# A sparse-attention and feed-forward kernel whose planner hands out PSUM banks by age, with a new order of all engines' work

## The chip, the cores and the metric

The kernel runs on one core of one Trainium2 chip. The metric is the device time of one launch in microseconds (us); below, "time" is this figure, and "span" is the stretch from the first to the last instruction in one profiled execution. The core's engines are named as in the profile: PE (TensorE, matrix products), DVE (VectorE), ACT (ScalarE), POOL (GpSimd), and SP, which here issues DMA transfers. Each engine works through its own list of instructions in order, and waits for others by semaphores. PE's results go to PSUM, a small store of eight banks of 512 float32 columns on 128 partitions, from which ACT or DVE must fetch them before a bank can be filled again.

## The reference

Four batches of eight heads, 768 positions, head size 64. Attention is masked by blocks of 32: neighbours, first and last block, and three sampled blocks for each query block. The result, 3,072 tokens of 512 values, goes through two weight matrices with a squared ReLU between them. Masking and softmax are in the attention part, relu and square in the second:

```python
scores = scale * np.matmul(q, k.transpose(0, 1, 3, 2))
scores = np.where(mask, scores, -1000000000.0)
scores = scores - np.max(scores, axis=-1, keepdims=True)
attn = np.exp(scores)
attn = attn / (np.sum(attn, axis=-1, keepdims=True) + 1e-09)
attn_out = np.matmul(attn, v)
x = attn_out.transpose(0, 2, 1, 3).reshape(B * S, H * D)
h = x @ w_in            # 512 -> 2048
r = np.maximum(h, 0.0)
g = r * r
return g @ w_out        # 2048 -> 512
```

## The kernel before

**Work and tiles.** Heads go in pairs: 16 pairs ("units"), four for each batch. For a pair, q and k are loaded as float32, cast to bf16 (`qc`), and transposed into `QK`: for the first batch by PE through PSUM (`transp`, `evac`), later by DMA (`transp_dma`, L402). v is cast into `VT`. Scores (L443) are computed with the keys on the partitions, 256 queries by two chunks of 128 keys for each of the two heads, which fills both banks of one X tile. ACT takes the exponential into `pT` (L454), DVE multiplies by a 0/1 mask (`MK`, L461), and PE multiplies with v (L483), with a column of ones that gives the sum. DVE normalises (L491, L493), and the result is transposed into `xT`. For the first 256 queries of the first batch the mask is added on PE instead (L447).

The second half takes a tile of 128, 256 or 384 tokens at a time. `hidden` (L541) fills one bank (512 columns; tiles of 128 and 256 tokens) or both banks of an X tile (768 columns; tiles of 384), in two or four parts. `relu` (L550 on ACT, L552 on DVE) brings it to SBUF as float32 `r`, `square` (L560 on ACT, L562 on POOL) makes `g`, and `output` (L585) multiplies by the second matrix, 16 matmuls for 128 tokens, into a bank of its own (`py`). A copy to `ys` (L246 on ACT, L248 on DVE or POOL) and a store end it.

**PSUM.** Three tiles X0 to X2 of 1,024 float32 columns, two banks each, are the shared store: scores and wide hidden groups need a whole tile ("X2" in the planner, two cells), and narrow hidden groups, first-batch transposes, mask tiles (L365) and some last outputs need one bank ("X1", one cell). One more bank serves `po`, one `py`.

**What sets the order.** The order is not written out. Every piece of work is a `Task` with a duration for each engine that may do it, a key (its rank), what it depends on, and the buffers that it takes (`get`) and gives back (`put`). `run_schedule` (L107) simulates the engines: again and again it takes the ready task that could start first, ties broken by the key, and emits it; so this model decides every engine's order, which engine does a piece, and which cells it uses. To the keys is added a pseudo-random number (`tie`, scaled by `TIES`, from one seed for every 64 tasks in `SEEDS`). `AHEAD` lets an urgent task be waited for. `LEAD` says how long before a unit's first scores its casts may begin, `PACE0` and `PACE` when each score group of the later batches may start. `arrive` lists when the model believes each load of the first batch to have landed. `bias` adds to a candidate engine's end when engines are compared, so a larger `bias` for ACT gives more of that work to DVE or POOL.

The function `bank` (L135) chooses a cell for a task that takes X1 or X2. Cells still held are left out; among the others the smallest `k_` wins: first the time `r` at which the task could use it, which is `now` for every cell that is free already, then, for one bank, a cell whose neighbour in the same tile is held, then the lowest number.

Of the kernel before, what the change touches and what calls it, by code (L numbers as in the profile page):

```python
# [25 lines left out]
def kernel(  # L26
# [21 lines left out]
    HP = H // 2  # L48
# [31 lines left out]
    LAT = {"PE": 0.23, "DVE": 0.06, "ACT": 0.06, "POOL": 0.08, "SP": 1.4}  # L80
    OVER = {"PE": 0.0, "DVE": 0.08, "ACT": 0.09, "POOL": 0.03, "SP": 0.0}
    SWITCH, SHARE, SLACK = 0.096, 0.85, 0.1
    AHEAD = {"PE": 0.043, "DVE": 0.108, "ACT": 0.176, "POOL": 0.0, "SP": 0.0}
    LEAD = 5.943
    HOLD = 0
    PACE0, PACE, SINGLE, MASK_AT = 39.28, 1.726, 1, 17.0

# [1 line left out]
    class Buf:  # L91
        def __init__(self, pool):
# [2 lines left out]

    TIES = 2.583, 1.777
    SEEDS = (
            621053, 621053, 621053, 162164, 486097, 621053, 621053, 88936, 279485,  # L100
            617998, 621925, 997023, 39474, 741514, 621053, 644142, 104467, 983473,
            256392, 272690, 973551, 604649, 254998, 99264)

    def tie(n):
        x = (n + 1) * 2654435761 & 0xFFFFFFFF ^ SEEDS[n // 64] * 2246822519 & 0xFFFFFFFF
# [18 lines left out]
    def run_schedule(free, bufs, dma_free, mode=128):  # L124
# [12 lines left out]
        def bank(pool, now, gone):  # L137
            n = 2 if pool == "X2" else 1
            best = None
            for c in range(0, 6, n):  # L140
                mine = [cells[i] for i in range(c, c + n)]
                if any(i in gone for i in range(c, c + n)) or any(b and b.holds for b in mine):
                    continue
                r = max([now] + [b.free for b in mine if b])
                o = cells[c ^ 1]
                k_ = (round(r, 4), n == 1 and not (o and o.holds), c)
                if best is None or k_ < best[0]:
                    best = (k_, c, r)
            return best

        relaxed = False
        while waiting or ready:
# [5 lines left out]
            now = [t for t in waiting if all(d.end is not None for d in t.deps)]  # L158
# [310 lines left out]
    def po_pool(u, q0):  # L469
        return "y" if u < HP and q0 < QW and (u + q0 // P) % 2 else "po"  # L470
# [127 lines left out]
    def T_(engs, key, f, *args, **kw):  # L598
        return Task(engs, key, (lambda e: f(*args, e)), **kw)
# [1 line left out]


    arrive = {(0, 1, 0): 3.4, (0, 0, 0): 4.2, (0, 1, CP): 4.55, (1, 0, 0): 5.7, (1, 1, 0): 6.7, (2, 0, 0): 7.2, (2, 1, 0): 8.3, (0, 2, 0): 9.4,
              (3, 0, 0): 9.8, (3, 1, 0): 10.9, (1, 2, 0): 12.4, (2, 2, 0): 13.5, (3, 2, 0): 14.6}
    arrive.update({(u, 0, 2): (15.5, 16.2, 16.8, 17.5)[u] for u in range(HP)})

    KEYS_OF = {P: [tuple(range(CP)), tuple(range(CP, NCH))], QW: [(2 * c, 2 * c + 1) for c in range(CP)]}
    OPEN = [(0, 0), (0, 1), (1, 0), (2, 0), (1, 1), (3, 0), (2, 1), (3, 1)]
# [56 lines left out]
    def attend(group, add):  # L665
        s = min(order.index(a) for a in group)
        bufs = {a: Buf("X2") for a in group}
        area = sum(a[2] * len(a[3]) for a in group) / 512
        deps = [ev[a[0]][1, n] for a in group for n in a[3]]
        deps += [ev[a[0]][0, n] for a in group for n in range(a[1] // P, (a[1] + a[2]) // P)]  # L670
        sc = T_(("PE", (0.44 if add else 0.22) * area), s, scores, group, add, bufs,
                deps=deps + (mr[:1 + (group[-1][1] + group[-1][2] > QW)] if add else []) + sc_all[-1:], get=[bufs[a] for a in group], mode=64,
                after=PACE0 + PACE * (s - N0) * (1.06 - 0.0006 * (s - N0)) if s >= N0 else 0.0, paced=group[0][1] >= QW or s >= N0)
        sc_all.append(sc)
        for i, a in enumerate(group):
            u, q0, w, cs = a
            sc_of[u].append(sc)
            s = order.index(a)
            part = w * len(cs) / 512
            pt = Buf("pT")  # L680
            ex = T_(("ACT", 0.2 + 0.82 * part), s, exps, a, deps=[sc], lead=sc.engs["PE"] * (len(group) - 1 - i) / len(group), get=[pt], put=[bufs[a]])
            if not add:
                ex = T_(("DVE", 0.68), s - 1, masks, a, deps=[ex] + [mk[n, c] for n in cs for c in range(q0, q0 + w, P)], port=True)
            if cs[0] == 0:
                ob[u, q0] = Buf(po_pool(u, q0))
            va = T_(("PE", 0.245 * part), s + 2.023, values, a, deps=[ex] + cv[u] + va_all[-1:] + (kws if po_pool(u, q0) == "y" else []),
                    get=[] if cs[0] else [ob[u, q0]], put=[pt], mode=128)
            va_all.append(va)
            va_of[u].append(va)
            if cs[-1] == NCH - 1:  # L690
                b, a_ = divmod(u, HP)
                by_dma = b > 0
                xqb = Buf("xq")
                nm = T_(("DVE", 0.3 + 0.16 * w / P), s - 9, normalize, u, q0, w, deps=[va], get=[xqb], put=[ob[u, q0]] if by_dma else [])
                kw = {}
                if b not in xb:
                    xb[b] = Buf("xT")
                    kw = dict(get=[xb[b]])
                if by_dma:
                    mu[u, q0] = T_(("SP", 1.22), s - 9, x_transp_dma, u, q0, w, deps=[nm], put=[xqb], dma=0.6, **kw)  # L700
                    continue
                xt = T_(("PE", 0.06 * w / P), s - 9, x_transp, u, q0, w, deps=[nm], put=[xqb], mode=128)
                mu[u, q0] = T_({"DVE": 0.11 + 0.09 * w / P, "ACT": 0.2 + 0.09 * w / P}, s - 9, x_evac, u, q0, w, deps=[xt], put=[ob[u, q0]], **kw)
# [10 lines left out]
    kws = []  # L714
# [28 lines left out]
    for k_, T in enumerate(TILES + [None]):  # L743
        hs = [(T, f) for f in range(0, NF, per_unit(T))] if T else []
        ys = [(TILES[k_ - 1], i, part) for i in range(len(y_tiles(TILES[k_ - 1]))) for part in range(NY)] if k_ else []
        both = [((i + 0.5) / len(hs), 0, x) for i, x in enumerate(hs)]
        both += [((i + 0.5) / len(ys), 1, x) for i, x in enumerate(ys)]
        for _, kind, x in sorted(both, key=lambda z: z[:2]):
            n_key += 1
            t = x[0]  # L750
            b, c0, w = t
            if kind == 0:
                f = x[1]
                need = [mu[b * HP + a, q0] for a in range(HP) for q0, qw in QT[b] if q0 < c0 + w and c0 < q0 + qw]
                w *= per_unit(t)
                wide = w > 512
                hb, rb = Buf("X2" if wide else "X1"), Buf("r")
                last_use = c0 + t[2] == S and f + per_unit(t) == NF
                parts = 4 if wide else 2
                hd = []  # L760
                for part in range(parts):
                    end = part == parts - 1
                    hd.append(T_(("PE", HID[w] / parts), n_key - (0.6 if part else 0.5), hidden, t, f, part, parts, hb,
                                 deps=hd[-1:] or need + [wl[f * NWP // NF], wl[(f + per_unit(t) - 1) * NWP // NF]],
                                 get=[] if part else [hb], put=[xb[b]] if last_use and end else [], mode=128, yields=not part))
                h1 = hd[-1]
                rr = T_(RELU[w], 200, relu, t, f, deps=[h1], get=[rb], put=[hb], bias={"ACT": 0.092})
                n = 1 if wide else per_unit(t)
                for i in range(0, per_unit(t), n):
                    gb = Buf("g")  # L770
                    gbuf[t, f + i + n - 1] = gb
                    sq = T_(SQ[n * t[2]], n_key, square, t, f, i, n, deps=[rr], get=[gb], put=[rb], bias={"ACT": 0.673})
                    sq_of.update({(t, f + i + j): sq for j in range(n)})
            else:
                _, i, part = x
                ts, cs = y_tiles(t)[i]
                n = (cs[1] - cs[0]) / d_model
                fs = range(part * NF // NY, (part + 1) * NF // NY)
                if part == 0:
                    yb = Buf(y_pool(t, i))  # L780
                last_i = i == len(y_tiles(t)) - 1
                yy = T_(("PE", 0.432 * n), n_key, output, t, i, ts, cs, part, yb,
                        deps=[sq_of[t, f] for f in fs] + [wl[NWP + f * NWP // NF] for f in fs] + ([yprev] if part else []),
                        get=[] if part else [yb], put=[gbuf[t, f] for f in fs if (t, f) in gbuf] if last_i else [], mode=128)
                yprev = yy
                if part == NY - 1:
                    sb = Buf("ys")
                    yc = T_({"ACT": 0.22 + 0.365 * n, "DVE": 0.15 + 0.53 * n}, 150, out_copy, t, i, cs, deps=[yy], get=[sb], put=[yb])
                    T_(("SP", 0.55), 0, store, t, i, ts, cs, deps=[yc], put=[sb], late=2.0, dma=0.7)
# [34 lines left out]
```

## Time and profile before

| what | us |
|---|---|
| time, median of 6 runs | 276.99 (276.83 to 278.73) |
| time of the profiled execution | 276.85 |
| its span | 275.1 |
| ACT busy, exponentials `pT` L454 | 137.9 (148 instructions) |
| ACT busy, relu L550 | 48.6 (65) |
| DVE busy, masks L461 | 93.3 (132) |
| PE, hidden L541 / output L585 to `py` | 640 / 328 matmul records |

The TensorE clock was granted in full throughout (1.000). Durations below come from the profiled execution, so a sum is made against its 276.85 us, of which 1.75 lie outside the span. Busy time on PE overlaps from one matmul to the next and some matmul records are missing, so PE's work is better read from start to start. A group's mean duration is taken by form where a line has several.

### The profile page before, as it was taken

To read this page: it belongs to the slowest core of one execution; us is meant where nothing else is said; L and a number is where in the kernel's file an instruction comes from. 1 tells how busy PE (TensorE), PEld (TensorE's weight loads), DVE (VectorE), ACT (ScalarE), POOL (GpSimd) and SP (SyncE) were. 2 spreads that over 40 slices of the span, in tenths; PEclk is the share of its full clock that TensorE was granted. 3 is DMA by queue.
4 is the path that set the end of the run, shared out by engine and by line. 5 is a ranking of instruction groups with operands and counts; after the bars stand their busy time and mean duration, and the time that the engine had idled before them with its cause. 6 is when DMAs were issued, how large, how long until landed. Compare 5 with 4: busy or idle time off the path is not lost.

```text
span 275.1 us, 7322 instructions
## 1 busy us (share of the span) xinstructions
PE 262.4 (95%) x2992; PEld 166.4 (61%) x3032; DVE 165.6 (60%) x339; ACT 224.2 (82%) x294; POOL 87.2 (32%) x110
## 2 busy tenths in 40 slices
PE   8989999889998999999999999999999999999995
PEld 5677665766566575556656556656565666555544
DVE  7777889734976988576847476685665555001010
ACT  3789999958997999999899989899798988646511
POOL 3192336345522035542221251312221122333210
PEclk9999999999999999999999999999999999999999
DMA  6999999999671239866670122443411011011112
GB/s 205 370 230 204 206 263 362 276 280 320 118 220 33 59 43 215 124 227 170 176 228 14 48 73 62 97 71 76 88 57 51 12 57 50 10 41 39 38 69 84
DMA packets 51881, 36.91 MB, mean 134 GB/s; under 512 B 30984, under 2 KB 48904, under 8 KB 51848
## 3 DMA queue, kind: packets, MB, share of 16 engines
q1 hardware_dynamic: 47080, 31.86, 43.5%
q0 software_dynamic: 4224, 4.19, 9.5%
q8 instruction: 23, 0.38, 0.5%
q10 hardware_dynamic: 544, 0.39, 0.5%
q14 instruction: 10, 0.08, 0.1%
HBM read 27.26 MB, written 6.29 MB: 122 GB/s over the span
## 4 chain that ended last, share of the span: by engine, by line
PE 86%; DVE 4%; ACT 3%; issue 2%; DMA 2%; SPq 1%; ACTq 0%; DVEq 0%
PE X L541 30%; PE py L585 27%; PE po L483 12%; PE X L443 12%; DMA ks<-in_k_dram 2%; PE X L585 2%; ACT r L550 1%; ACT pT L454 1%; DVE pT L461 1%; DVE QK L248 1%; SPq L274 1%; PE X L365 1%; PE po L500 1%; PE X L395 1%; PE X L447 0%
## 5 line engine op out<-in xcount | busy, mean ns | idle before, releaser
L454 ACT ACTIVATE pT<-X 128x1024 bf16<-128x1024 f32 (+1 forms) x148 | 137.9, 1006 | 8.1 <-PE X L443 5.3
L461 DVE TENSOR_TENSOR pT<-pT,MK 128x1024 bf16<-128x1024 bf16 x132 | 93.3, 727 | 24.4 <-ACT pT L454 23.7
L562 POOL TENSOR_TENSOR g<-r 128x384 bf16<-128x384 f32 (+1 forms) x65 | 59.2, 914 | 151.4 <-ACT r L550 129.5
L541 PE MATMUL X<-xT,w_in_sb 128*128 128x384 bf16 (+2 forms) x640 | 99.9, 294 | 2.9 <-ACT r L550 2.5
L585 PE MATMUL py<-w_out_sb,g 128*128 128x512 bf16 (+1 forms) x328 | 87.6, 374 | 3.4 <-issue 1.9
L541 PEld LDWEIGHTS <-w_in_sb 128*128 128x128 bf16 x640 | 54.3, 97 | 33.3 <-issue 6.7
L550 ACT ACTIVATE r<-X 128x768 f32<-128x768 f32 (+1 forms) x65 | 48.6, 754 | 22.4 <-PE X L541 19.7
L483 PEld LDWEIGHTS <-pT 128*128 128x128 bf16 x1152 | 47.4, 98 | 17.8 <-issue 4.2
L483 PE MATMUL po<-VT,pT 128*128 128x65 bf16 x1152 | 53.4, 194 | 0.1
L585 PEld LDWEIGHTS <-g 128*128 128x128 bf16 x400 | 34.3, 98 | 27.8 <-issue 4.4
L443 PE MATMUL X<-QK 64*128 64x256 bf16 (+1 forms) x624 | 46.8, 264 | 0.5
L443 PEld LDWEIGHTS <-QK 64*128 64x128 bf16 x624 | 26.1, 94 | 18.8 <-issue 14.2
L560 ACT ACTIVATE g<-r 128x384 bf16<-128x384 f32 (+1 forms) x55 | 29.7, 540 | 3.0 <-DVE r L552 1.4
L491 DVE RECIPROCAL rs<-po 128x4 f32<-128x4 f32 (+1 forms) x52 | 9.3, 178 | 35.7 <-PE po L483 35.6
L248 DVE COPY ys<-py 128x512 f32<-128x512 f32 x17 | 11.7, 685 | 27.6 <-PE py L585 27.6
L493 DVE TENSOR_TENSOR xq<-po,rs 128x256 bf16<-128x256 f32 (+1 forms) x52 | 21.0, 404 | 1.8
L248 POOL CAST VT<-vs 128x768 bf16<-128x768 f32 x15 | 15.7, 1048 | 18.7 <-issue 11.2
L248 DVE CAST qc<-ks 128x768 bf16<-128x768 f32 (+1 forms) x15 | 11.3, 755 | 0.8 <-DMA ks<-in_k_dram 0.7
L248 DVE CAST qc<-qs 128x768 bf16<-128x768 f32 (+2 forms) x16 | 9.1, 571 | 0.2 <-DMA qs<-in_q_dram 0.2
L246 ACT COPY ys<-py 128x512 f32<-128x512 f32 (+1 forms) x6 | 3.3, 558 | 5.5 <-PE py L585 5.3
L447 PE MATMUL X<-R,oh 64*128 64x128 bf16 x96 | 6.9, 219 | 0.0
L585 PE MATMUL X<-w_out_sb,g 128*128 128x512 bf16 (+1 forms) x32 | 6.0, 326 | 0.0
(54 smaller groups left out, 76.2 us busy)
## 6 DMA issues: line engine op xcount, KB each, us to landing
vs<-in_v_dram SPq DMA_DIRECT2D x16, 384.0 KB, 6.6
out_dram<-ys SPq DMA_DIRECT2D x23, 256.0 KB, 2.2
ks<-in_k_dram SPq DMA_DIRECT2D x15, 384.0 KB, 4.9
qs<-in_q_dram SPq DMA_DIRECT2D x12, 384.0 KB, 3.9
w_in_sb<-in_moe_w_in_dram POOLq DMA_DIRECT2D x4, 512.0 KB, 8.6
w_out_sb<-in_moe_w_out_dram POOLq DMA_DIRECT2D x4, 512.0 KB, 15.0
qs<-in_q_dram SPq DMA_DIRECT2D x4, 256.0 KB, 7.2
xT<-xq SPq DMA_TRANSPOSE x36, 2.3
```

What stands on the lines that cost most here:

```text
L248: (V if e == "DVE" else G).tensor_copy(out=out, in_=in_)
L443: nc.tensor.matmul(ps[:, h, j * w:(j + 1) * w], QK[i][hs, 1, ksl], QK[i][hs, 0, qsl], start=j == 0, stop=not add, skip_group_check=True)
L454: A.activation(out=pT[:, :, 0:n], in_=stile.pop(a)[:, :, 0:n], func=AF.Exp, scale=scale)
L461: V.tensor_tensor(out=pT, in0=pT, in1=m[:, None].broadcast_to([P, 2, len(cs), w]), op=AOP.mult)
L483: nc.tensor.matmul(po[:, qc, h, :], pT[:, h, j * w + qc * P:j * w + (qc + 1) * P], VT[i][:, h, n, 0:VW], start=(n == 0 and qc == 0 and h = ...
L491: V.reciprocal(out=rs, in_=po[:, :, :, D:VW])
L493: V.tensor_tensor(out=xq, in0=po[:, :, :, 0:D], in1=rs.broadcast_to([P, n, 2, D]), op=AOP.mult)
L541: nc.tensor.matmul(htile[T, f][:, i], w_in_sb[:, kc, (f + i) * P:(f + i + 1) * P], xT[b][:, kc, c0:c0 + w], start=(kc == 0), stop=(kc == K ...
L550: A.activation(out=to, in_=src, func=AF.Relu)
L560: A.activation(out=g, in_=r, func=AF.Square)
L562: (G if e == "POOL" else V).tensor_mul(out=g, in0=r, in1=r)
L585: nc.tensor.matmul(ytile[T, i], gtile[T, f][:, ts * P:(ts + 1) * P], w_out_sb[:, f, cs[0]:cs[1]], start=(f == 0), stop=(f == NF - 1))
```

## The change

In `bank`, the first term of the choice is no longer the time at which a cell can be used, but that of the cell's release plus 0.8 us, or `now` if that is later. Cells that came free over 0.8 us ago are equal; among fresher ones the one that was released first is taken. The time at which the task may start is worked out as before. The loads of v for units 1 to 3 and the second parts of q are believed to land 0.4 to 1.0 us later. The other numbers steer the model: `AHEAD`, `LEAD` (5.943 to 9.349), `PACE0`, the shift of the value matmuls' key, and ACT's biases for relu (0.092 to 0.192) and square (0.673 to 0.8). New `TIES` and `SEEDS` give a new order. All of these act before the program is built; none adds an instruction to it. Line numbers after `bank` grow by one.

```diff
-    AHEAD = {"PE": 0.043, "DVE": 0.108, "ACT": 0.176, "POOL": 0.0, "SP": 0.0}
-    LEAD = 5.943
+    AHEAD = {"PE": 0.045, "DVE": 0.057, "ACT": 0.278, "POOL": 0.0, "SP": 0.0}
+    LEAD = 9.349
     HOLD = 0
-    PACE0, PACE, SINGLE, MASK_AT = 39.28, 1.726, 1, 17.0
+    PACE0, PACE, SINGLE, MASK_AT = 40.983, 1.721, 1, 17.0
...
-    TIES = 2.583, 1.777
+    TIES = 1.511, 0.048
     SEEDS = (
-            621053, 621053, 621053, 162164, 486097, 621053, 621053, 88936, 279485,
...
+            309547, 309547, 309547, 309547, 65971, 309547, 309547, 729044, 629699,
...
                 r = max([now] + [b.free for b in mine if b])
                 o = cells[c ^ 1]
-                k_ = (round(r, 4), n == 1 and not (o and o.holds), c)
+                old = max([now] + [b.free + 0.8 for b in mine if b])
+                k_ = (round(old, 4), n == 1 and not (o and o.holds), c)
...
-              (3, 0, 0): 9.8, (3, 1, 0): 10.9, (1, 2, 0): 12.4, (2, 2, 0): 13.5, (3, 2, 0): 14.6}
-    arrive.update({(u, 0, 2): (15.5, 16.2, 16.8, 17.5)[u] for u in range(HP)})
+              (3, 0, 0): 9.8, (3, 1, 0): 10.9, (1, 2, 0): 13.4, (2, 2, 0): 14.5, (3, 2, 0): 15.4}
+    arrive.update({(u, 0, 2): (16.1, 16.7, 17.3, 17.9)[u] for u in range(HP)})
...
-            va = T_(("PE", 0.245 * part), s + 2.023, values, a, deps=[ex] + cv[u] + va_all[-1:] + (kws if po_pool(u, q0) == "y" else []),
+            va = T_(("PE", 0.245 * part), s + 2.994, values, a, deps=[ex] + cv[u] + va_all[-1:] + (kws if po_pool(u, q0) == "y" else []),
...
-                rr = T_(RELU[w], 200, relu, t, f, deps=[h1], get=[rb], put=[hb], bias={"ACT": 0.092})
+                rr = T_(RELU[w], 200, relu, t, f, deps=[h1], get=[rb], put=[hb], bias={"ACT": 0.192})
...
-                    sq = T_(SQ[n * t[2]], n_key, square, t, f, i, n, deps=[rr], get=[gb], put=[rb], bias={"ACT": 0.673})
+                    sq = T_(SQ[n * t[2]], n_key, square, t, f, i, n, deps=[rr], get=[gb], put=[rb], bias={"ACT": 0.8})
```

More of the change, by code (lines that the diff above doesn't have):

```diff
@@ L93, in __init__ @@
             self.pool, self.holds, self.free, self.at = pool, 0, 0.0, None
-    TIES = 2.583, 1.777
+    TIES = 1.511, 0.048
     SEEDS = (
-            621053, 621053, 621053, 162164, 486097, 621053, 621053, 88936, 279485,
-            617998, 621925, 997023, 39474, 741514, 621053, 644142, 104467, 983473,
-            256392, 272690, 973551, 604649, 254998, 99264)
+            309547, 309547, 309547, 309547, 65971, 309547, 309547, 729044, 629699,
+            29976, 309547, 521787, 731003, 309547, 309547, 787178, 309547, 792806,
+            298466, 671173, 309547, 137610, 309547, 309547)
     def tie(n):
```

## The prediction

> **What bounds the kernel now.** I read the page's busy line first, then the slices, the chain of waits, PE's waits, the windows by stage, and last the timeline around PE's longest stops.
>
> ```profile
> PE 262.4 (95%) x2992; PEld 166.4 (61%) x3032; DVE 165.6 (60%) x339; ACT 224.2 (82%) x294; POOL 87.2 (32%) x110
> ...
> PE   8989999889998999999999999999999999999995
> ...
> DVE  7777889734976988576847476685665555001010
> ACT  3789999958997999999899989899798988646511
> ...
> PE 86%; DVE 4%; ACT 3%; issue 2%; DMA 2%; SPq 1%; ACTq 0%; DVEq 0%
> ```
>
> PE is busy from the first slice to the last and carries 86% of the chain. Ninety-five per cent busy doesn't tell how much PE time could go, so I counted PE's work by its issue intervals. The chain shows them:
>
> ```profile
> 248.00 1.30 PE X L541 x8
> 249.30 2.16 PE py L585 x10
> ```
>
> That is 162 ns for a hidden matmul of 384 columns and 216 ns for an output of 512. In the same way, from start to start in the timeline: 109 ns for 256 columns, 56 for 128, 30 for a value matmul, 54 for each of a pair of 256-column score matmuls, and 190 ns extra for going into a run of scores and out again. Times their counts in the program (384 x 162, 128 x 109 and 128 x 56 hidden; 368 x 216 and 32 x 109 out; 1,152 x 30 values; the scores, transposes and masks) the products make 245.0 us, and 74 runs of scores add 13.9: **258.9 us**. I call the running sum of these PE's position. PE starts at 1.2 us and its last matmul goes out near 271.6, so some 11.6 us are stops. Setting each PE start in the trace against its position gives where: 4.0 us up to position 20, 3.8 from 20 to 50, 2.4 from 50 to 90, and 1.4 in the remaining 170 us. Beyond position 90 there is next to nothing to win.
>
> ```profile
> PE X L541 <- ACT r L550: 2.5, 4, 0.8
> ...
> 52.00:62.00 10.00, 8.20 (x85) 6.10 (x84) 4.65 (x9) 6.79 (x13) 5.05 (x5) 1.00 1.06 265
> ...
> 57.55 0.60 PE L541 MATMUL X<-xT,w_in_sb 128*128 128x256 bf16 x4
> 58.18 0.60 ACT L550 ACTIVATE r<-X 128x512 f32<-128x512 f32 x1 [0.50 <-PE X L541]
> 58.83 0.60 PE L541 MATMUL X<-xT,w_in_sb 128*128 128x256 bf16 x4 [0.69 <-ACT r L550]
> ```
>
> The first line (waiter, releaser, total us, times, longest) is PE's largest entry: four stops, at 53.55, 58.83, 60.11 and 85.69, which by starts cost 0.97 + 0.86 + 0.37 + 0.88 = 3.1 us. The window from 52 to 62 is where PE is least busy, and there ACT (6.79) and DVE (4.65) are idle too: nobody is overloaded, they take turns. The three timeline lines show how. Four matmuls, then ACT's relu, then the second four matmuls of the same group. In the built order that relu reads the other half of the X tile that PE is writing. It waits for PE's latest write to that tile, and PE's next part waits for the relu. So the two banks of one X tile are not independent in this program, although the planner's model keeps six separate cells.
>
> **What the Trainium skill says.** The Trainium skill, page "PSUM — Partial Sum Buffer", section "PSUM bank collisions raise a hardware error", asks for a guard by bank; reads and writes of different banks may run together. The trace shows a stricter guard here: PE at 58.83 waits 0.69 us for a read of the neighbouring bank. Its page "Perfetto Trace Analysis", section "Identifying the Most-Contended Engine", says that matmul busy time is a poor measure of headroom; I agree, and took issue intervals. Its page "ScalarE: Activation LUTs", section "Rules for kernel authors", wants relu on VectorE. Here the rows say otherwise for this operand: a 768-wide relu out of PSUM takes 958 ns on DVE (one case) and 812 on ACT.
>
> **The change, part by part.**
>
> *PE.* The same instructions, and 74 runs of scores in both: 258.9 us again. What differs is who waits.
>
> *Work moved between engines* (counts from both built orders, durations from the rows by form). ACT loses 14 relus of 768 columns (14 x 0.812), 3 of 512 (3 x 0.600), 3 squares (0.52 + 2 x 0.63) and one x copy, and gains 3 output copies (3 x 0.595) and one QK copy (some 0.4): -13.1 us. DVE gains 14 x 0.958 + 3 x 0.686 and loses 3 x 0.685 of output copies and a cast or so: +13.0. POOL gets some 2.6 more. This looks large and is worth little. Twelve of the fourteen wide relus come after the last scores, where slices 35 to 40 have DVE at 0 or 1 and ACT at 6 and below; there PE returns to a bank 3.4 to 5.6 us after filling it, against 0.96 for the relu. I cost them at nothing. Were that cover gone, each would cost its extra 0.15 us, 1.8 in all.
>
> *Which bank is taken.* For every PE wait on a reader of an X tile I took the room: PE work between the last matmul that the reader waits for and the waiting one. A wait has no margin when the room is under the reader's duration and some 0.3 us for the two signals; it is exposed to a short queue when under duration and 0.6.
>
> | PE position, us | waits exposed, before / after | sum short, before / after, us |
> |---|---|---|
> | 0-20 | 13 / 20 | 0.59 / 0.94 |
> | 20-50 | 10 / 10 | 1.58 / 1.59 |
> | 50-90 | 8 / 3 | 1.15 / 0 |
> | 90-259 | 22 / 9 | 0.15 / 0.54 |
>
> Four waits of before on the other half of a tile are short by 0.79, 0.79, 0.36 and 0.79, 2.73 us together; they are the four stops that the trace has at 3.08. After, those four are gone, and three new ones stand at positions 45.5, 48.4 and 49.8 with 0.68 + 0.36 + 0.44 = 1.48. At the same ratio of 1.13 they cost 1.67: **-1.4 us**. Elsewhere the start is worse by 0.35, and around position 116 a hidden group takes a bank with a room of 1.01 against an exp of 1.03, and three more are short by 0.08: **+0.35 and +0.4**.
>
> *Queues.* ACT is what PE waits for from 20 to 50 (19.58 us busy of 20 between 22 and 42). Adding up ACT's durations in order until the last instruction that PE needs gives, at position 38, 41.0 before and 39.4 after; at 50, 54.1 and 52.1; at 90, 94.1 and 92.5. Two of the 2.0 us at 50 are relus and squares that now stand later or on DVE. Some of the 6.2 us lost between 20 and 90 is that queue: 6.2 less the 3.1 of the four stops. Bounds: 0, if DVE takes ACT's place, and -2.0; I take **-0.8**, since the excess of ACT's sum over PE's position grows from 20 to 46 by 4.8 us before and 3.8 after.
>
> *Later landings in the model.* No instruction. They put v casts and values later in the start, where the trace has v of the second to fourth pair landing at 12.5, 13.5 and 14.8 us against 13.4, 14.5 and 15.4 in the new list: margin, within the start's +0.35. Bounds -0.5 and +1.5 (below).
>
> *Casts 3.4 us earlier (LEAD).* Smallest room from a batch's cast to the scores that use it: 9.3 us before, 9.9 after, against a transpose of 2.8 to landing. The loads have more than 10 us before any cast from the second batch on. Nothing. The last stores are issued in the same order, so the tail of 3.3 us stays.
>
> Sum: -1.4 + 0.35 + 0.4 - 0.8 = -1.45. The profiled execution took 276.85 us (span 275.1), 0.14 under the median of 276.99: **275.4 us**.
>
> **Rivals.**
> - *Stops only move, 276.6.* DVE's additions cancel the queue's gain and the start costs 0.7: -1.4 + 0.7 + 0.4 = -0.3. For it: banks free for over 0.8 us still tie, and the tie still goes to the half-held tile, so "oldest first" bites only on fresh banks; waits on a neighbour half even rise from 21 to 33. That is also the case that the change doesn't do what it says. Against: the rooms from 50 to 90.
> - *Slower, 278.7: DVE decides the start.* Its sum up to what PE needs is 27.2 after against 25.7 at position 22 (one more 768 cast, one more mask) and 43.4 against 40.3 at 38. DVE is busy 17.14 of 20 us from 22 to 42, so 2.9 us of idle time may cover it, or be waits that stay. If under 1.3 us of that idle time can be used, 1.5 us at 22 and 1.0 more by 38 come through: -1.4 + 0.35 + 0.4 + 2.5 = +1.85.
> - *All cover holds, 273.3.* From 20 to 90 only the three half-tile stops and 1.0 us of small waits remain of 6.2: -3.5.
>
> **How the numbers follow.** Forecast 0.46, stops move 0.22, slower 0.21, full cover 0.11. Changes under 0.5% (1.4 us) I count as none, about what a measurement of this kernel can tell. The forecast is at -0.57%, and I leave a fifth of its chance to no change: faster 0.37 + 0.11 = 0.48, same 0.22 + 0.09 = 0.31, slower 0.21. Its own range is 274.4 to 276.4; the full range takes in most of both outer cases, 273.4 to 278.4.
>
> **What would show it.** Right: no PE stop near 85 us, three between 50 and 62 of 0.2 to 0.6 us after r; PE's X waits on r from 2.5 to some 1.5 us; ACT near 211 and DVE near 179 us busy; POOL idle, tail and chain end as before. Wrong on the start: the first batch's hidden matmuls, which stand at position 20.4 after 19.9, begin later than about 26.3 us against 25.4, with DVE at 9 in the slices before. Wrong on the queue: the window from 22 to 42 loses more PE time than the 0.6 us of now. A stop of over 1 us beyond 100 us, or a DMA landing among PE's releasers, would upset the forecast altogether.

## The result, and the profile after

The changed kernel takes 278.43 us (median of 36 runs, 277.73 to 279.80); the kernel before, run beside it, 277.25 (73 runs). The ratio is 1.0039, with a 95% interval of 1.0029 to 1.0049: some 1.1 us slower, where 1.45 us faster was forecast. The profiled execution has a span of 276.6 us against 275.1. (One correction to the text above: in the listing `run_schedule` begins at L124 and `bank` at L137.)

The page of the changed kernel: the busy line, three of the slices, the chain.

```profile
PE 263.5 (95%) x2994; PEld 165.2 (60%) x3032; DVE 179.1 (65%) x353; ACT 211.1 (76%) x277; POOL 90.7 (33%) x113
...
PE   7899999789999999999999999999999999999995
...
DVE  7776999836997886767565657567576565434400
ACT  3779898746998999999879799998979988223111
...
PE 76%; ACT 7%; DVE 7%; DMA 3%; issue 3%; SPq 2%; POOL 1%; ACTq 0%; DVEq 0%
```

ACT and DVE stand where the counting put them (211 and 179), DVE partly by luck, as told below. The chain has changed: PE carries 76% of it in place of 86%, ACT and DVE together 14% in place of 7%. In the PE line the eighth slice (48 to 55 us) has a 7 in place of an 8.

PE's waits after 45 us in the changed kernel (waiter, releaser, total us, times, longest; the four largest), and then PE's timeline at the four stops that matter:

```profile
PE X L542 <- ACT r L551: 1.2, 2, 0.9
PE po L484 <- DVE xT L249: 0.9, 1, 0.9
PE po L484 <- DVE pT L462: 0.5, 1, 0.5
PE X L542 <- DVE r L553: 0.4, 1, 0.4
```

```profile
51.40 0.89 PE L484 MATMUL po<-VT,pT 128*128 128x65 bf16 x24 [0.90 <-DVE xT L249]
...
55.56 0.60 PE L542 MATMUL X<-xT,w_in_sb 128*128 128x256 bf16 x4 [0.94 <-ACT r L551]
...
58.94 0.60 PE L542 MATMUL X<-xT,w_in_sb 128*128 128x256 bf16 x4 [0.31 <-ACT r L551]
...
60.94 1.03 PE L542 MATMUL X<-xT,w_in_sb 128*128 128x256 bf16 x8 [0.42 <-DVE r L553]
```

The stop at 85 us is gone and three remain behind a relu, as forecast, though larger than forecast. The stop for `xT`, which DVE copies, was not foreseen, nor was one of 0.45 us for a mask multiply (`pT`), at 92.27. Measured from start to start, the four in the timeline cost 1.07, 1.10, 0.48 and 0.53 us, to some 0.05 us.

Where the time went is read best from PE's lag: the time at which a matmul starts less its position (the running sum of PE's work from the prediction). What the lag grows by in a stretch is what PE lost there, in us (a row is good to some 0.05):

| PE position | before | after | later casts | list, order before | list, order after |
|---|---|---|---|---|---|
| 0-10 | 3.78 | 4.01 | 3.98 | 3.30 | 3.79 |
| 10-24.5 | 2.34 | 3.07 | 3.06 | 2.06 | 2.66 |
| 24.5-40 | 0.70 | 0.72 | 0.73 | 1.95 | 0.99 |
| 40-57 | 2.63 | 3.34 | 2.28 | 0.24 | 0.92 |
| 57-95 | 2.05 | 1.43 | 1.43 | 1.47 | 1.00 |
| 95-end | 1.28 | 1.64 | 1.63 | 2.64 | 2.32 |
| sum | 12.78 | 14.21 | 13.11 | 11.66 | 11.68 |

The first two columns differ by +1.43: +0.23 and +0.73 in the start, +0.71 from 40 to 57, -0.62 to 95 (the stop at 85 us is gone, the one at 92.27 is new), +0.36 in the rest. The other columns are experiments below. Each column is one execution. The first row moves by itself: two kernels whose first 196 steps are the same had 4.01 and 4.90 there, according to when the first loads land.

### The profile page after: what moved, and what is told of

Read it like the earlier page. It is cut to its first block, busy times and chain, and to the rows that moved or that the text cites. A ratio compares the mean times of both kernels' runs of the same rounds, so it can differ in the third digit from the quotient of the medians.

```text
span 276.6 us, 7334 instructions
## 1 busy us (share of the span) xinstructions
PE 263.5 (95%) x2994; PEld 165.2 (60%) x3032; DVE 179.1 (65%) x353; ACT 211.1 (76%) x277; POOL 90.7 (33%) x113
## 4 chain that ended last, share of the span: by engine, by line
PE 76%; ACT 7%; DVE 7%; DMA 3%; issue 3%; SPq 2%; POOL 1%; ACTq 0%; DVEq 0%
PE X L542 29%; PE py L586 24%; PE po L484 11%; PE X L444 10%; ACT pT L455 4%; DVE pT L462 4%; DMA vs<-in_v_dram 3%; ACT r L551 2%; PE X L586 2%; SPq L275 2%; DVE xq L494 1%; DVE r L553 1%; DVE QK L249 0%; POOL g L563 0%; ACT ys L247 0%
## 5 line engine op out<-in xcount | busy, mean ns | idle before, releaser
L563 POOL TENSOR_TENSOR g<-r 128x384 bf16<-128x384 f32 (+1 forms) x68 | 63.9, 943 | 147.0 <-ACT r L551 103.2
L462 DVE TENSOR_TENSOR pT<-pT,MK 128x1024 bf16<-128x1024 bf16 x132 | 97.7, 762 | 15.2 <-ACT pT L455 14.8
L484 PE MATMUL po<-VT,pT 128*128 128x65 bf16 x1152 | 55.9, 194 | 1.7 <-DVE xT L249 0.9
L561 ACT ACTIVATE g<-r 128x384 bf16<-128x384 f32 (+1 forms) x52 | 27.8, 537 | 24.4 <-DVE r L553 23.2
L551 ACT ACTIVATE r<-X 128x768 f32<-128x768 f32 (+1 forms) x48 | 35.6, 745 | 11.3 <-PE X L542 10.2
L553 DVE TENSOR_SCALAR r<-X 128x768 f32<-128x768 f32 (+1 forms) x24 | 20.5, 856 | 23.5 <-PE X L542 22.0
L249 POOL CAST VT<-vs 128x768 bf16<-128x768 f32 x14 | 13.5, 965 | 20.8 <-issue 9.9
L247 ACT COPY ys<-py 128x512 f32<-128x512 f32 (+1 forms) x9 | 5.1, 570 | 10.7 <-PE py L586 10.5
L249 DVE COPY ys<-py 128x512 f32<-128x512 f32 x14 | 9.6, 685 | 2.7 <-PE py L586 2.7
L249 DVE CAST qc<-ks 128x768 bf16<-128x768 f32 (+1 forms) x13 | 7.9, 605 | 1.3 <-DMA ks<-in_k_dram 1.3
```

What stands on the lines that cost most here:

```text
L249: (V if e == "DVE" else G).tensor_copy(out=out, in_=in_)
L462: V.tensor_tensor(out=pT, in0=pT, in1=m[:, None].broadcast_to([P, 2, len(cs), w]), op=AOP.mult)
L484: nc.tensor.matmul(po[:, qc, h, :], pT[:, h, j * w + qc * P:j * w + (qc + 1) * P], VT[i][:, h, n, 0:VW], start=(n == 0 and qc == 0 and h = ...
L551: A.activation(out=to, in_=src, func=AF.Relu)
L553: V.tensor_scalar(out=to, in0=src, scalar1=0.0, scalar2=None, op0=AOP.max)
L561: A.activation(out=g, in_=r, func=AF.Square)
```

## The experiments

All kernels compute the whole output. Each replays a written list of steps in place of the simulation: a task's number, the letter of its engine, and the bank for a task that takes one. Line numbers are those of the kernel before. The kernel before ran again beside each set, with medians of 277.25 to 277.61 us; so differences come from the ratios, taken of 277.25 us, unless medians are named.

**1. The bank rule alone, in both directions.** The order is kept and the rule exchanged.

```diff
 # order of before with this edit (first run); order of after without it (second run)
-                k_ = (round(r, 4), n == 1 and not (o and o.holds), c)
+                k_ = (round(old, 4), n == 1 and not (o and o.holds), c)
```

> The order of the kernel before, step for step on every engine; only the PSUM banks are handed out oldest first, as the changed kernel does. Full computation. In the model the stops for a bank that is still being read fall from 5.3 to 4.4 us, nearly all of it before position 20 and between 50 and 90. Theory (the new order costs the time, the bank rule saves): 0.4 to 0.9 us less than the kernel before, ratio 0.997 to 0.9985. Rival (the bank rule is what costs): 0.7 us or more above the kernel before, ratio 1.003 or more.

> The order of the changed kernel, step for step; the PSUM banks are handed out by the rule of the kernel before (lowest number that is free). Full computation. In the model the bank stops are 5.4 us in place of the 4.1 of the changed kernel. Theory (order costs, bank rule saves): about 1.3 us above the changed kernel, some 279.5 us, ratio to the kernel before 1.008. Rival (the bank rule costs): below the changed kernel, ratio to the kernel before 1.001 or less.

Measured: order before with banks by age 276.87 us, ratio 0.9983 (0.9963 to 1.0003); order after with banks by number 279.36 us, 1.0084 (1.0062 to 1.0106). The second is 1.2 us above the changed kernel, as expected, and its interval lies clear of it. The first is 0.5 below the kernel before, with an interval that just takes in no change. So the bank rule isn't what costs time. With the old rule in both, the new order takes 2.3 us more than the old one: the order costs.

**2. The start alone.** The first 196 steps are the same tasks in both orders (six of them on other engines), so they can be exchanged whole. Behind them the tasks keep the order of their kernel, but some banks differ: 29 steps in the first run and 18 in the second take other banks than in the kernel that the rest comes from.

```diff
 # first run: steps 1-196 of before, then 197-1491 of after; second run: the other way round
-193A 817P4 ...
+817P4 193A ...
```

> The first 196 steps of the schedule (to position 24.5 of PE's work) in the order and with the banks of the kernel before, all the rest as in the changed kernel. Full computation. Theory (the start is where the order loses 1.0 to 1.3 us): about 1.0 us below the changed kernel, 277.4 us, ratio to the kernel before 1.000 to 1.001, and the lag of PE at position 24.5 is 6.1 us. Rival (the loss lies in the middle, at the stop near 51 us): within 0.3 us of the changed kernel, ratio 1.003 to 1.005.

> The first 196 steps of the schedule in the order and with the banks of the changed kernel, all the rest as in the kernel before. Full computation. Theory (the start loses): about 1.0 us above the kernel before, some 278.2 us, ratio 1.0035, and the lag of PE at position 24.5 is 7.1 us. Rival (middle): within 0.3 us of the kernel before. If this run and the one with the starts the other way round don't add up to the difference of the two kernels, the parts aren't independent.

Measured: start of before 278.08 us, ratio 1.0027 (1.0010 to 1.0045); start of after 278.90 us, 1.0056 (1.0036 to 1.0076). Both go the way of the theory, but not by its size: the start of after costs 1.6 us in front of the old rest, and the start of before wins only 0.3 in front of the new, with an interval that overlaps the changed kernel's. So the two runs don't add up to the difference of the kernels. For each of them the trace shows a stop that is not due to the order of the start.

In the profile of the kernel with the start of after, the lag grows by 2.09 us from position 24.5 to 40, where it grows by 0.70 in the kernel before. Some 0.6 of this is one stop of a score group that takes the tile of the score group before it (banks 0 and 1 are one tile, 2 and 3, 4 and 5), so that it waits for that group's exponential. The kernel before has another tile there, and no stop:

```diff
 # two score groups, the same tasks between them: the kernel before, then this run
-254P2 ... 258P4
+254P0 ... 258P0
```

```profile
43.72 0.39 PE L443 MATMUL X<-QK 64*128 64x256 bf16 x4 [0.54 <-ACT pT L454]
```

It isn't that the old rest begins late: the first kernel of experiment 4 gives both groups one tile too (254P4, 258P4), its PE comes there 0.4 us earlier than in the kernel before, and it has the same stop:

```profile
41.12 0.39 PE L443 MATMUL X<-QK 64*128 64x256 bf16 x4 [0.54 <-ACT pT L454]
```

The kernel with the start of before has, in its profiled execution (279.03 us, above its median), a stop of 1.30 us at 24.57 that no engine's lateness explains; it is taken up in the last section. Less that stop, its lag grows by 2.37 us from 10 to 24.5, as in the kernel before (2.34), and the 196 steps of after give 3.07 in both kernels.

**3. DVE beside POOL.** Before the stop at 51.4, DVE's queue in the changed kernel, then POOL's (start, busy us, operation; a row may hold several instructions):

```profile
46.17 2.52 DVE L462 TENSOR_TENSOR pT<-pT,MK 128x1024 bf16<-128x1024 bf16 x2
48.61 0.17 DVE L492 RECIPROCAL rs<-po 128x4 f32<-128x4 f32 x1
48.81 0.42 DVE L494 TENSOR_TENSOR xq<-po,rs 128x256 bf16<-128x256 f32 x1
49.16 1.99 DVE L462 TENSOR_TENSOR pT<-pT,MK 128x1024 bf16<-128x1024 bf16 x2
51.07 0.28 DVE L249 COPY xT<-po 128x256 bf16<-128x256 bf16 x1
```

```profile
46.09 0.82 POOL L249 CAST VT<-vs 128x768 bf16<-128x768 f32 x1
46.86 1.29 POOL L249 CAST qc<-ks 128x768 bf16<-128x768 f32 x1
48.10 1.28 POOL L249 CAST qc<-qs 128x768 bf16<-128x768 f32 x1
49.33 1.28 POOL L249 CAST VT<-vs 128x768 bf16<-128x768 f32 x1
```

Three of the four mask multiplies take 1.3 us in place of 0.68, and three of the four casts 1.28 in place of 0.82. The copy of `xT` stands behind the multiplies on DVE, and PE stands behind the copy. The Trainium skill, page "SBUF — State Buffer", section "Who interferes with whom", says that a DVE instruction with two inputs in SBUF contends with a GpSimd instruction that reads SBUF. The trace agrees as to the pair of operations; one multiply and one cast side by side take 1.29 us, less than their 1.50 us one after the other. So three casts, with the two transposes and the load that follow them, were put behind POOL's next square:

```diff
-300G 301S ... 302G ... 303S ... 310G ... 473S ... 835G ... 850S
+835G 300G 302G 310G ... 850S 301S 303S 473S
```

> The changed kernel with three casts on POOL (q and k of pair 4, v of pair 5) and the transposes and the load that follow them moved behind POOL's next square, so that they no longer run beside DVE's mask multiplies between 46 and 51 us. Full computation, same banks. Theory (DVE and POOL slow each other there, and the stop of 1.07 us near 51.4 us comes from it): the mask multiplies between 46 and 51 us take 0.7 us in place of 1.3, the stop falls under 0.3 us, the time falls by 0.7 to 0.9 us against the changed kernel, ratio to the kernel before 1.001. Rival (the stop follows from the order of DVE's own work): the stop stays above 0.8 us and the ratio at 1.004. If the transposes now land too late, a new stop of PE stands between 63 and 68 us, at the first scores of the second batch.

Measured: 277.75 us, ratio 1.0007 (0.9982 to 1.0033), 0.9 us less than the changed kernel (0.7 by the medians). DVE's timeline in this kernel:

```profile
46.14 1.89 DVE L461 TENSOR_TENSOR pT<-pT,MK 128x1024 bf16<-128x1024 bf16 x2
48.20 0.18 DVE L491 RECIPROCAL rs<-po 128x4 f32<-128x4 f32 x1 [0.18 <-PE po L483]
48.42 0.42 DVE L493 TENSOR_TENSOR xq<-po,rs 128x256 bf16<-128x256 f32 x1
48.76 1.28 DVE L461 TENSOR_TENSOR pT<-pT,MK 128x1024 bf16<-128x1024 bf16 x2
49.97 0.28 DVE L248 COPY xT<-po 128x256 bf16<-128x256 bf16 x1
```

Two multiplies take 1.28 us together, the copy begins 1.1 us earlier, and PE's stop there is gone. One multiply is still slow, at 46.14, beside the v cast that was left in place. No stop over 0.2 us appears from 62 to 83 us, so the transposes land in time. In the table the row 40-57 falls by 1.06 and no other row changes by more than 0.03. Traffic on the DMA engines is not the cause: from 47 to 50 us their share is 1.07 with slow multiplies and 1.06 with fast ones. By the ratios this contention is 0.9 of the 1.1 us that the change costs. The two ratios' intervals just touch (0.9982 to 1.0033, 1.0029 to 1.0049); the trace, where one stop goes and no other row moves, carries the rest.

**4. The half-tile stops.** The order of the kernel before with a list of banks that sends PE to another tile. For the eight hidden groups that begin between positions 42 and 53:

```diff
-838P1 844P2 851P3 856P0 861P0 866P1 871P0 876P1
+838P0 844P3 851P4 856P5 861P1 866P5 871P1 876P5
```

> The order of the kernel before, step for step on every engine; the banks are given out by a fixed list, searched offline so that PE goes to another tile than the one whose other half is still being read. Full computation. Theory (the four stops of 0.4 to 1.0 us after a relu come from two halves of one tile being guarded as one): those four stops are gone, PE's waits on r for X fall from 2.5 us to under 0.5, and the time is 2.5 to 3.0 us less than the kernel before, ratio 0.989 to 0.991. Rival (ACT's queue is late there whatever the bank): the stops stay or come back within 10 us of PE's work, and the time is within 1 us of the kernel before.

Measured: 275.74 us, ratio 0.9922 (0.9896 to 0.9948), 2.2 us less, where 2.5 to 3.0 were expected. PE's window from 52 to 62 us is full (9.95 of 10 us; 8.20 in the kernel before), and in PE's waits after 45 us no relu is left:

```profile
PE py L585 <- issue: 1.9, 12, 0.2
PE X L541 <- ACT pT L454: 0.5, 3, 0.2
PE X L443 <- DVE MK L373: 0.3, 1, 0.3
PE py L585 <- POOL g L562: 0.2, 1, 0.2
```

In the steps of the kernel before, the relu that each stop waits for reads the other half of the tile: 851P3 waits for the relu of 844P2, 866P1 for that of 861P0, 871P0 for that of 866P1, 920P3 for that of 912P2. So the mechanism of the forecast is shown: the four stops come from two halves of one tile being guarded as one. Less was won than they cost (3.07), since two places give some back: 1.25 us from position 24.5 to 40, with the score stop shown under 2, and 1.36 after 95. (All rows together give 1.1 us, the difference of the two profiled executions; that of the kernel before, 276.85, lies below its medians.) The loss after 95 is four stops of 0.25 to 0.35 us at positions 107, 158, 173 and 188; three of them are the second line above.

The same for the order of after:

```diff
-838P5 844P0 851P1 856P0 861P1 866P0 871P2 876P1
+838P3 844P5 851P0 856P2 861P1 866P5 871P1 876P2
```

> The order of the changed kernel, step for step on every engine; banks by a fixed list searched offline as for the order of the kernel before. Full computation. Theory (half-tile stops): the three stops near 55.6, 58.9 and 60.9 us (2.1 us together) are gone and the time is 2.0 to 2.4 us below the changed kernel, some 276.2 us, ratio to the kernel before 0.995 to 0.997; the stop of 1.07 us near 51.4 us stays, since no bank causes it. Rival (ACT's queue): within 1 us of the changed kernel.

Measured: 275.95 us, ratio 0.9941 (0.9925 to 0.9958), 2.5 us below the changed kernel by the medians and 2.7 by the ratios, slightly more than expected. The three stops are gone; the one for `xT` stays, at 0.64 us.

**5. What the start is made of.** Two attempts at the engines that do the work, one at its banks.

```diff
 # first run
-50D
+50G
 # second run
-90D 78D 92A 94A 39A 50D
+90A 78A 92D 94D 39D 50G
 # third run, in the first 196 steps only
-                k_ = (round(old, 4), n == 1 and not (o and o.holds), c)
+                k_ = (round(r, 4), n == 1 and not (o and o.holds), c)
```

> The changed kernel with one instruction moved: the cast of v of pair 2 goes from DVE to POOL, where the kernel before has it, between the loads of the first matrix. Full computation, same banks, all else in the same order. Theory (DVE decides the start): 0.4 to 0.6 us less than the changed kernel, ratio to the kernel before 1.002. Rival (the start is lost through the order of PE's own work): within 0.2 us of the changed kernel, ratio 1.004.

> The order and banks of the changed kernel; six instructions of the start (four copies of mask tiles, one of transposed q and k, one cast of v) go to the engines that do them in the kernel before, at the same place of the order. Full computation. Theory (which engine does what decides the start): the lag of PE grows by 2.2 to 2.5 us from position 10 to 24.5 in place of 3.07, time 0.5 to 0.8 us less than the changed kernel, ratio 1.001 to 1.002. Rival (the order of PE's work decides): lag still 3.0 us or more, ratio 1.004.

> The order of the changed kernel; the banks are handed out by lowest number in the first 196 steps (to position 24.5) and oldest first from there on. Full computation. Theory (in the start the old rule suits the new order better): the lag grows by 2.5 us from position 10 to 24.5 in place of 3.07, and the time is 0.3 to 0.6 us less than the changed kernel, ratio 1.002 to 1.003. Rival (the order of PE's work decides, whatever the banks): within 0.2 us of the changed kernel, ratio 1.004.

Measured: 278.77 us, ratio 1.0041 (1.0021 to 1.0060), with the v cast on POOL; 278.70, 1.0042 (1.0027 to 1.0057), with all six on their old engines; 278.73, 1.0047 (1.0032 to 1.0063), with the old bank rule in the start. None wins anything, so all three theories failed. The lag grows from 10 to 24.5 by 3.07, 2.83 and 3.26 us (the last with some 0.4 of waiting for a v cast on POOL). So neither the engine that copies a tile or casts v nor the bank rule explains the loss. What remains is the order of the work itself; this is argued by leaving out the rest, and not shown, and whether PE's order or that of another engine decides stays open.

**6. Putting the gains together.** The stops at 107 to 188 have a reason that the first lists overlooked. There PE fills three tiles with scores, ACT empties them one after the other, and two hidden groups follow. In the kernel before, the second of them takes the tile of the second exponential; under the first list it took that of the third:

```diff
 # three tiles of scores; hidden group; hidden group (order before; first list, then second)
-509P042 ... 993P0 ... 1002P2
+509P240 ... 993P2 ... 1002P4
```

In the profile with the first list, ACT's run of three exponentials and PE's wait for the last of them:

```profile
114.03 2.85 ACT L454 ACTIVATE pT<-X 128x1024 bf16<-128x1024 f32 x3 [0.26 <-PE X L443]
```

```profile
116.93 0.49 PE L541 MATMUL X<-xT,w_in_sb 128*128 128x384 bf16 x2
```

The three exponentials end 0.92 us apart, the third at 116.88, and the second hidden group begins at 116.93. After position 50 both lists were searched again with this counted.

> The order of the changed kernel with the three casts moved as in the run with later casts, and the fixed list of banks as in the run with the changed order; after position 50 the list is searched again, counting that ACT's exponentials of one run of scores end 0.93 us apart. Full computation. Theory (the gains add: 0.9 for the casts, of which 0.4 was already won by the banks, 2.7 for the banks, 0.5 more for the two late stops at 128 and 169 that the first list brought): 274.3 to 274.8 us, ratio to the kernel before 0.988 to 0.991, no PE stop over 0.35 us between 45 and 270 us. Rival (what is won is given back at the next engine that is late): 275.7 us or more, ratio 0.993 or more.

> The order of the kernel before, with the fixed list of banks searched again after position 50 as in the other run of this pair. Full computation. Theory (the late stops of 0.25 to 0.33 us at positions 107, 158, 173 and 188 of the first list came from hidden groups that took the tile of the third exponential in place of the second): they are gone, and the time is 1.0 to 1.3 us below the run with the first list, 274.4 to 274.8 us, ratio to the kernel before 0.987 to 0.989. Rival (ACT's queue is the limit there once PE is earlier): stops of the same sum stay, 275.5 us or more, ratio 0.992.

Measured: order of after, casts moved, new list, 275.76 us, ratio 0.9912 (0.9882 to 0.9943); order of before, new list, **274.73 us, ratio 0.9904 (0.9871 to 0.9936)**, by the medians 2.5 us under the kernel before and 3.7 under the changed one. This is the fastest found, and within the 274.4 to 274.8 us expected; its ratio lies just above the 0.987 to 0.989. With only six runs each the intervals are wide: the second lies 1.0 us below its first list by the medians, but the ratios overlap, so the step is shown by the trace rather than by the time. Its profile is that of its slowest run (277.06; the other five took 274.54 to 275.34), with 1.6 us more lag in the start than the kernel before, 1.04 of it a stop of the kind described at the end. After position 95 the lag grows by 1.54 us in place of 2.64, and PE's waits after 45 us are down to:

```profile
PE py L585 <- issue: 1.9, 12, 0.2
PE X L541 <- ACT pT L454: 0.2, 1, 0.2
PE py L585 <- POOL g L562: 0.2, 1, 0.2
```

The run with the order of after missed its expectation of 274.3 to 274.8: after position 45 it has one stop over 0.35 us, 0.44 at 89.89, but in the start of its profile a wait of 1.2 us for a v cast on POOL.

## Why the prediction was wrong

It forecast 275.4 us; 278.43 came. Against its own profile the sum was -1.45, and the lag grew by +1.43. Step by step:

- *Counts, engines, no added work*: right in the counts. ACT's 211.1 us are as worked out. DVE's 179.1 fit the 178.6 partly by luck: the masks took 4.4 us more, which was not forecast, and the k casts on DVE 3.4 us less, where "a cast or so" was. POOL rose by 3.5 against 2.6.
- *Half-tile stops, -1.4*: right in mechanism and place, and shown by the lists of banks. The size was off. The four of before are 3.07 us; the three of after 1.10 + 0.48 + 0.53 = 2.11 against 1.67 forecast, so -0.96. The first of them carries most of the miss: 0.68 x 1.13 = 0.77 was forecast for it.
- *Start, +0.35*: too small. It was +0.96 by position 24.5, of which 0.23 lies where the landing of the first loads moves it anyway. The first hidden matmuls of the first batch begin at 26.91 us, beyond the 26.3 that the text named as the sign. The term came from rooms at banks only, and the old bank rule in the start wins nothing.
- *Position 116 and later, +0.4*: right. The stop at 116 is 0.28 us, and all that follows position 95 is +0.36.
- *Queues, -0.8*: this is the step that failed, together with *casts, nothing*. What the other terms leave is 1.43 - (-0.96 + 0.96 + 0.36) = +1.07, as much as the stop at 51.40 (the new stop at 92.27 and some smaller differences cancel). The bounds of the step were 0 and -2.0, so it fell outside both. ACT's queue was shorter, but at 51.40 PE waited for DVE, and there it won nothing. The step on the casts asked whether their data would be in time, and found 9.9 us of room. It didn't ask what the casts do to DVE while they run. In the kernel before they ran from 43.3 to 47.3 us, beside three multiplies of 0.90, 0.77 and 0.96 us where 0.68 is usual; in the changed kernel they ran from 46.1 to 50.6 beside four multiplies, three of them at 1.3. The stretch was there to be read in the trace of before, at 0.6 us in this place:

```profile
44.48 0.90 DVE L461 TENSOR_TENSOR pT<-pT,MK 128x1024 bf16<-128x1024 bf16 x1
...
45.84 0.77 DVE L461 TENSOR_TENSOR pT<-pT,MK 128x1024 bf16<-128x1024 bf16 x1
46.88 0.96 DVE L461 TENSOR_TENSOR pT<-pT,MK 128x1024 bf16<-128x1024 bf16 x1 [0.27 <-ACT pT L454]
```

```profile
43.25 0.82 POOL L248 CAST VT<-vs 128x768 bf16<-128x768 f32 x1 [1.02 <-DMA vs<-in_v_dram]
44.02 0.83 POOL L248 CAST qc<-ks 128x768 bf16<-128x768 f32 x1
44.79 1.28 POOL L248 CAST qc<-qs 128x768 bf16<-128x768 f32 x1
46.28 1.02 POOL L248 CAST VT<-vs 128x768 bf16<-128x768 f32 x1 [0.21 <-DMA vs<-in_v_dram]
```

The kernel's own listing names the pair too: in `run_schedule` a mask or cast on DVE (`port=True`) and any task on POOL are lengthened by 0.85 (`SHARE`) of the time that they overlap.

The pages have the sum over the whole kernel, for the same 132 multiplies, before and after:

```profile
L461 DVE TENSOR_TENSOR pT<-pT,MK 128x1024 bf16<-128x1024 bf16 x132 | 93.3, 727 | 24.4 <-ACT pT L454 23.7
L462 DVE TENSOR_TENSOR pT<-pT,MK 128x1024 bf16<-128x1024 bf16 x132 | 97.7, 762 | 15.2 <-ACT pT L455 14.8
```

That is 762 ns for one in place of 727, 4.4 us more on DVE. A count of instructions does not show it, since their number is the same.

Of the rivals, "slower, 278.7: DVE decides the start" came within 0.3 us and named the right engine, but not the place, so that it came so close was luck. From position 24.5 to 40 nothing more was lost (0.72 after 0.70), and giving the start's work back to its old engines won nothing. DVE decided later, at 51 us, and only where POOL ran beside it.

Two things stay open: what in the order of the start loses the 0.73 us from position 10 to 24.5, and how much of the 1.6 and 0.3 us of the exchange is the start and how much the two other stops found there.

## What to carry to other kernels

Before a planner's new order is believed, look for stretches where two engines that slow each other run side by side, and price each pair from a row of the trace. Here a queue that got shorter on paper won nothing, since the next engine in line got slower there. Where several banks share one guard, choose a bank by which tile's reader finished longest ago in that reader's own order, counting that one engine empties the tiles one after the other. On the order of the kernel before, this took off 2.5 us by the medians. When a schedule is cut in two to find where it loses, keep the banks of each part as they were, or the run tests two things at once.

## What the runs showed of the hardware

**PE stops where a block of its instructions is fetched.** PE's timeline at the 352nd matmul of the program, in three kernels whose first 196 steps have the order of before: the kernel before, the one with banks by age, and the one with the start of before and the rest of after:

```profile
23.20 0.61 PE L443 MATMUL X<-QK 64*128 64x256 bf16 x8
```

```profile
23.49 0.61 PE L443 MATMUL X<-QK 64*128 64x256 bf16 x8 [0.44 <-issue]
```

```profile
24.57 0.61 PE L443 MATMUL X<-QK 64*128 64x256 bf16 x8 [1.30 <-ACT pT L454]
```

The releaser in the last row is not the cause of the whole stop: ACT's signal was there at 23.80, 0.77 us before PE went on, and the wait began at 23.3. The page of the kernel before lists a queue of kind "instruction", with 23 packets of 16 KB; the line above it is the share of the DMA engines in 40 slices, in tenths:

```profile
DMA  6999999999671239866670122443411011011112
...
q8 instruction: 23, 0.38, 0.5%
```

By the packet table the second of the 16 KB packets that fall within the span starts at 20.87, 21.24 and 22.05 us in these three. Two more profiles have a stop at the 352nd matmul, of 0.23 us (packet at 21.16, the order of after) and 1.04 us (22.48). From the start of the packet to the matmul it is 2.25 to 2.52 us in all four that stop. Where the packet starts by 20.9 us, or PE comes later (packet at 22.02, matmul at 24.40), no stop is seen. The stop thus follows the fetch of the next block of instructions, in the fourth slice, where the DMA engines stand at 9. The Trainium skill, page "Runtime: NRT & Kernel Launch", section "Instruction fetch mechanics", has the blocks of 16 KiB, and says that the cost of crossing into the next is mostly hidden. Here a stop of up to 1.3 us goes with it, and it changes from one run to the next. It may be a part of the spread of these kernels (277.24 to 280.57 us for the one with 1.30); no run took the load off the DMA engines to see whether the stop goes. So neither that nor the load as its cause is shown.
